# Reordering the chunk loop of RWKV-7 with a squared-ReLU FFN: state decay, state turn, squares and loads at other places in a slot

## The chip, the cores and the metric

The kernel runs on one core of a Trainium2 chip, in float32. The metric is the device time of one execution in microseconds (us). Five engines of the core work side by side, each through its own list of instructions in order: TensorE (PE, matrix products and transposes, with its weight loads as PEld), VectorE (DVE), ScalarE (ACT), GpSimd (POOL) and SyncE (SP, which here only issues DMA transfers). They wait for each other by semaphores.

## The reference

The first half is a recurrence over 768 time steps for 4 batches of 8 heads with 40 channels each; the second half is an FFN over the 3072 resulting rows of 320.

```python
for t in range(S):                       # per batch and head, state is D x D
    y[t]  = einsum('d,de->e', r[t], state)
    Sa    = einsum('de,e->d', state, a[t])
    state = state * w[t] - outer(Sa, b[t]) + outer(v[t], k[t])
x = y.transpose(0, 2, 1, 3).reshape(B * S, H * D)
h = maximum(x @ w_in, 0)                 # 320 -> 2048
out = (h * h) @ w_out                    # 2048 -> 320
```

## The kernel before

**Tiling.** Time is cut into chunks of 128 steps. There are 24 chunks, taken in the order "all four batches of chunk 0, then all four of chunk 1" and so on, so that neighbours in the order belong to different batches; `order[i]` holds batch and chunk. The main loop has one *slot* per chunk, numbered 0 to 23. In slot i three kinds of work are put side by side:

- the *chain* of chunk i (`chain`, L600): products of the state with the chunk's decayed a (first `xw`), a transpose, products with the inverse T and the block N, the new rows turned back, the growth of the state (`grown`, added by DVE in L662), the masked products RX, and the output y, which DVE scales into `tokens` (L683). From there it is regrouped by small SBUF-to-SBUF DMAs for the FFN.
- the *preparation of chunk i+1*: `turn_rv` transposes r and v; `make_rv` makes the products RV and masks them on DVE (L332); `turn_k` transposes k and scales it with the decay `dec` into `kvT` (L510); `decay_state` multiplies the state of chunk i+1's batch with the decay accumulated since (L533, L536); `turn_down` and `scale_kb` scale k and b (L551); `make_a` makes and masks the products A; `turn_state` transposes the state on PE (L561) and ACT copies it to `sd` (L563). The state decayed here belongs to another batch than the one that chain i grows.
- *early work on later chunks* (`early`, called through `prepare`): scans and reciprocals of the decays, products N, and their stores to DRAM (`kept_e`, `kept_d`, `kept_n`). It is present in slots 0 to 14 and gone from slot 15 on. POOL inverts the blocks of several chunks at a time (`solving`), loading `kept_d` and storing `kept_t`; its results come back as T.

Between these stand pieces of the FFN (`Ffn`): `thirds` and `whole` are the first product (w_third, w_in) with ReLU on ACT, `square` squares the hidden rows on DVE (L742), `make_quarter` is a quarter of the second product (w_out). In slot 4 alone the last weights are still being converted (`halves`, from `rounding`), using the same PSUM buffers (`ps_f`, two of them) as `thirds`; `extra` then places additional FFN pieces, in slot 4 only.

**What sets the order.** The order is written out by hand. Slots 0 to 3 weave generators in fixed proportions (`woven`, with `rest` for the next chunk). From slot 4 on `sorted_slot` (L909) lists the calls one by one; each `step` runs its calls and then lets stores that are due go out (`tick`). Every engine executes its instructions in the order of these calls. `ps_w`, a pool of four PSUM buffers, takes turns among all transposes and masked products; `ps_c`, with two, among the chain's.

**Loads.** SP issues in order. For chunk i+1 the keys k, the decays `dec` (634 KB from `kept_e`) and b are issued by `loads` at the head of slot i, r and v for chunk i+2 within it (`fetch_next`, L905). `dec` has two buffers, of which the one loaded was last read by DVE in L683; k, b and v have two each, r has one.

Of the kernel before, what the change touches and what calls it, by code (L numbers as in the profile page):

```python
# [11 lines left out]
Alu = mybir.AluOpType  # L12
# [5 lines left out]
def kernel(  # L18
# [73 lines left out]
    def new(name, shape, bufs):  # L92
        return work.tile(shape, FP32, tag=name, name=name, bufs=bufs)
# [413 lines left out]
    def turn_k(i, g):  # L507
        kT, kT_ = turned("kvT", 1), turn(g["x"]["k"])
        down = g["dec"][:, DOWN]
        nc.vector.tensor_tensor(kT, kT_, down[:, :, 1:C + 1], Alu.mult)  # L510
        g["kT"], g["ends"] = kT, new("ends", [128, NP], 2)
        nc.vector.tensor_copy(g["ends"], down[:, :, 0])

    def make_a(i, g):
        g["A"] = masked("A", 2, g["kT"], g["aT"])
# [1 line left out]
    def turn_rv(i, g):  # L517
        x_ = g["x"]
        while "v" not in x_:
            line.pop(0)[1]()  # L520
        g["rT"], g["vT"] = turned("rT", 2), turned("kvT", 1)
        p_, p2_ = turn(x_["r"]), turn(x_["v"])
        nc.scalar.copy(g["rT"], p_)
        nc.scalar.copy(g["vT"], p2_)
        g["v"] = x_["v"]

    def decay_state(i, g):
        bb, c = order[i]
        if c == 0:
            return  # L530
        st = states.tiles[bb]
        f_ = new("f", [128, NP], 1)
        nc.vector.tensor_tensor(f_, ended[bb], g["ends"], Alu.mult)  # L533
        for e in range(2):
            own_ = st[e * DP:(e + 1) * DP, :, e, :D]
            nc.vector.tensor_tensor(own_, own_, f_[e * DP:(e + 1) * DP].unsqueeze(2).to_broadcast([DP, NP, D]), Alu.mult)  # L536
# [32 lines left out]
    def rest(i, g):  # L569
        begin(i, g)  # L570
        yield
        yield
        turn_k(i, g)
        joining = inverses(i, g) if i else iter(())
        if soon(i):
            next(joining, None)
        yield
        make_a(i, g)
        yield
        turn_rv(i, g)  # L580
        yield
        decay_state(i, g)
        make_rv(i, g)
        if i and unit_of[i] < FINE:
            next(joining)
        yield
        turn_down(i, g)
        yield
        scale_kb(i, g)
        turn_state(i, g)  # L590
        yield
        yield from joining
        yield
# [6 lines left out]
    def chain(i, g):  # L600
        bb, c = order[i]
        st = states.tiles[bb]
        first, second_ = slice(0, HC), slice(HC, C)
        low, high = slice(0, DP), slice(DP, 128)

        xw = quads(psum(ps_c))
        for h, q, e, rows in heads:
            mm(xw[rows, q], g["v"][:, h, :], g["A"][e][:, q], h < 2)
        yield
        if c > 0:  # L610
            for q in range(NP):
                mm(xw[:, q], st[:, q].rearrange("p e d -> p (e d)"), g["aT"][:, q], False)
        xc = turned("xnT", 1)
        nc.scalar.copy(xc[low], xw[low])  # L614
        for n in range(2):
            nc.scalar.copy(xc[high, :, n * HC:(n + 1) * HC], xw[high, :, (1 - n) * HC:(2 - n) * HC])
        yield

        p_ = psum(ps_c)
        for q in range(NP):  # L620
            nc.tensor.matmul(p_[:, q * 128:(q + 1) * 128], xc[:, q], ident, start=q == 0, stop=True, is_transpose=True,  # L621
                             skip_group_check=True)
        x_ = p_.rearrange("t (h d) -> t h d", h=H)[:, :, :D]
        xr = new("xr", [128, H, D], 1)
        nc.scalar.copy(xr, x_)
        yield
        T, N = g["T"], g["N"]
        xn = minus_x.next()
        halves = (first, second_)

        def times_t(half):
            xs = psum(ps_c)[:, :NP * D].rearrange("p (q d) -> p q d", q=NP)
            for h, q, e, _ in heads:
                rows = halves[half ^ e]
                mm(xs[rows, q], T[rows, order_of(h)], xr[rows, h], h < 2)
            nc.scalar.copy(xn[halves[half], ::2, :D], xs[halves[half]])
            nc.scalar.copy(xn[halves[half], 1::2, :D], xs[halves[1 - half]])  # L637

        times_t(0)
        yield  # L640
        for h, q, e, _ in heads:
            mm(x_[halves[1 - e], h], N[:, order_of(h)], xn[first, h, :D], False)
        nc.scalar.copy(xr[second_, ::2], x_[second_, ::2])
        nc.scalar.copy(xr[first, 1::2], x_[first, 1::2])
        yield
        times_t(1)
        yield
        p_ = psum(ps_c)
        for q in range(NP):
            nc.tensor.transpose(p_[:, q * 128:(q + 1) * 128], pair(xn, q), ident)  # L650
        xT = turned("xnT", 1)
        nc.scalar.copy(xT, quads(p_))
        yield
        k_, b_, v_, rT = (g[x] for x in ("k", "b", "v", "rT"))
        if c < NCH - 1:
            grown = psum(ps_c)[:, :NP * 2 * D].rearrange("p (q d) -> p q d", q=NP)
            for l_, r_ in ((k_, v_), (b_, xn)):
                for q in range(NP):
                    mm(grown[:, q].rearrange("p (e d) -> p e d", e=2), pair(l_, q), r_[:, 2 * q:2 * q + 2, :D], l_ is k_ and q == 0)
            for e in range(2):  # L660
                rows = slice(e * DP, (e + 1) * DP)
                nc.vector.tensor_tensor(st[rows, :, e, :D], grown[rows, :, e * D:(e + 1) * D], st[rows, :, e, :D], Alu.add)  # L662
            ended[bb] = new(f"end{bb}", [128, NP], 1)
            nc.vector.tensor_copy(ended[bb], g["up"][:, :, C])
        yield
        rx = masked("RX", 2, xT, rT)
        yield

        y_ = quads(psum(ps_c))
        if c > 0:  # L670
            sd = g["sd"]
            for q in range(NP):
                mm(y_[:, q], sd[:, q].rearrange("p e d -> p (e d)"), rT[:, q], q == 0)
        yield
        for m_, rows in ((g["RV"], k_), (rx, b_)):
            for q in range(NP):
                for e in range(2):
                    mm(y_[e * DP:(e + 1) * DP, q], rows[:, 2 * q + e, :], m_[e][:, q], c == 0 and q == 0 and rows is k_)
        n = i % GB
        if n == 0:  # L680
            tokens[i // GB] = new("tokens", [128, NP, GB * C], 2)
        t_ = tokens[i // GB][:, :, n * C:(n + 1) * C]
        nc.vector.tensor_tensor(t_, y_, g["up"][:, :, :C], Alu.mult)  # L683
        if n == GB - 1:
            t_ = tokens[i // GB]
            for j, row, h, d, m_ in moves:
                at = (h % 2) * DP + d
                store(t_[row:row + m_, j], t_[at:at + m_, h // 2], 1)
            later(lambda: gathered.add(i // GB), 2)
        yield  # L690
# [214 lines left out]
    def fetch_next(i, *names):  # L905
        if i < len(order):
            loaded.setdefault(i, {}).update({nm: fetch(nm, {"k": k, "b": b, "r": r, "v": v}[nm], i) for nm in names})

    def sorted_slot(i, g, ch):  # L909
        j = i + 1  # L910
        more = j < len(order)
# [16 lines left out]
        def extra():  # L928
            if not begun:
                second.thirds()  # L930
                second.whole()

        halves = lambda: [next(rounded, None) for _ in range(2)] if not begun else None

        def loads():
            if more:
                fetch_next(j, "k")
                n["dec"] = kept_here[j % 2]
                nc.sync.dma_start(out=n["dec"][:USED], in_=kept_e[j])
                fetch_next(j, "b")  # L940

        loads()
        step(on(ch), halves)
        if more:
            begin(j, n)
# [3 lines left out]
            next(joining, None)  # L949
        fetch_next(j + 1, "r")  # L950
        step(second.make_quarter, halves)
        extra()
        step(on(ch))
        step(of(make_rv), second.thirds)
        step(on(ch), on(one), on(two), on(two))
        if fine:
            next(joining, None)
        step(second.whole, on(two))
        step(on(ch))
        step(on(one), of(turn_k))  # L960
        step(on(ch), of(decay_state), on(one), of(turn_down), of(scale_kb))
        step(on(ch), of(turn_state), second.square)
        if fine:
            next(joining, None)
        step(on(ch), of(make_a), second.thirds, on(one))
        fetch_next(j + 1, "v")
        step(second.whole, on(two), on(two))
        if not early_join:
            next(joining, None)
        step(on(ch), extra)  # L970
# [1 line left out]
        if more:  # L972
            later_chain = n["chain"] = chain(j, n)
            next(later_chain)
        run(ch)
        step(second.square, second.make_quarter)
        step(second.make_quarter, on(two))
        for gen in (one, two, joining):
# [2 lines left out]
    for i in range(len(order)):  # L981
# [4 lines left out]
        if i < B:  # L986
            woven(i, g, ch)
            n = ready[i + 1]
            n["chain"] = chain(i + 1, n)
            next(n["chain"])  # L990
            if i == B - 1:
                fetch_next(i + 2, "r", "v")
        else:
            sorted_slot(i, g, ch)
        while unit < len(units) and all(m_ in done for m_ in range(len(order)) if unit_of[m_] == unit):
# [46 lines left out]
```

## Time and profile before

| | |
|---|---|
| median of three runs | 1095.37 us (1087.47 to 1097.03) |
| profiled execution | 1094.95 us, span 1093.2 us |
| PE busy | 952.3 us, 87% of the span |
| PE weight loads (PEld) | 785.3 us, 72% |
| DVE busy | 491.6 us, 45% |
| ACT busy | 284.4 us, 26% |
| POOL busy | 669.4 us, 61% |
| DMA | 106.92 MB, mean 98 GB/s |
| TensorE clock granted, mean | 0.87 of full |

The profile is one execution. Busy time of PE is modelled at its ends, so a full PE can still hide some slack; the waits ahead of an instruction, and what released it, tell more than the sums. "PE ps_w L87" names matrix products into the buffers `ps_w`, issued by the helper in line 87; many products share that line and are told apart by their tiles. "DVE RX L332" after an arrow is what ended a wait. Slots 0 to 3 take the first 250 us or so, slots 4 to 14 run to about 725 us, slots 15 to 23 to about 1016 us, and the rest is FFN alone.

### The profile page before, as it was taken

The page shows a single profiled execution, that of the slowest core. Times are in us where ns is not written, and L with a number is a line of the kernel's source. Part 1 is how long each engine was busy: PE and PEld are TensorE (multiplying, and loading weights), DVE is VectorE, ACT ScalarE, POOL GpSimd, SP SyncE. Part 2 cuts the span into 40 slices and gives each one's busy share as a digit, 9 for nine tenths or more (in the row PEclk, how much of TensorE's full clock was granted, in tenths as well). Part 3 has the DMA queues.
Part 4 walks back from the last instruction along what each step waited for, and adds up shares of the span by engine and source line. Part 5 has one row for each costly group of instructions (what it writes and reads, how often), then busy time and mean ns, then how long its engine had stood idle before and what let it go on. Part 6 is the DMA issues. An engine that isn't in the chain of part 4 may idle for free.

```text
span 1093.2 us, 19699 instructions
## 1 busy us (share of the span) xinstructions
PE 952.3 (87%) x7728; PEld 785.3 (72%) x7728; DVE 491.6 (45%) x908; ACT 284.4 (26%) x643; POOL 669.4 (61%) x1128
## 2 busy tenths in 40 slices
PE   6275765685899899999899999999999999999998
PEld 5264654674788787778677877878888887777776
DVE  5456683784554435537246345344323433231111
ACT  3133241332231322222312222212222222322111
POOL 4788544886885399993699976999768810000000
PEclk8666575566998898999988998989999999999999
DMA  8878969678144862654873655541644314230000
GB/s 109 145 141 165 174 168 177 147 150 138 43 82 108 143 118 58 98 98 117 142 125 58 100 132 110 95 85 26 136 90 84 65 37 92 47 63 7 13 13 12
DMA packets 261376, 106.92 MB, mean 98 GB/s; under 512 B 244100, under 2 KB 250372, under 8 KB 259620
## 3 DMA queue, kind: packets, MB, share of 16 engines
q1 hardware_dynamic: 256756, 86.65, 44.4%
q0 software_dynamic: 3440, 18.88, 7.5%
q8 instruction: 61, 1.00, 0.4%
q10 hardware_dynamic: 1088, 0.13, 0.1%
q14 instruction: 31, 0.25, 0.1%
HBM read 72.47 MB, written 31.19 MB: 95 GB/s over the span
## 4 chain that ended last, share of the span: by engine, by line
PE 66%; DVE 12%; DMA 8%; issue 4%; ACT 4%; POOL 3%; SPq 2%; ACTq 0%; DVEq 0%; POOLq 0%
PE ps_f L87 36%; PE ps_c L87 13%; PE ps_w L87 11%; PE ps_w L316 4%; DMA in_w<-in_w_dram 2%; DMA dec<-kept_e 2%; DVE hid L742 1%; SPq L108 1%; DVE state L536 1%; PE ps_c L621 1%; POOL half_t L450 1%; POOL half_p L448 1%; DVE RX L332 1%; DMA blocks<-kept_t 1%; DVE kvT L510 1%
## 5 line engine op out<-in xcount | busy, mean ns | idle before, releaser
L448 POOL TENSOR_TENSOR half_p<-half_n,half_t 128x70 f32<-128x70 f32 (+52 forms) x502 | 296.7, 591 | 101.5 <-DMA half_n<-kept_d 51.8
L450 POOL TENSOR_TENSOR half_t<-half_t,half_p 128x70 f32<-128x70 f32 (+52 forms) x502 | 323.4, 644 | 39.3
L87 PE MATMUL ps_f<-w_out,hid 128*128 128x320 f32 x768 | 221.0, 438 | 0.0
L87 PEld LDWEIGHTS ps_f<-w_out,hid 128*128 128x128 f32 x768 | 142.0, 191 | 54.9 <-issue 4.4
L87 PE MATMUL ps_f<-tokens,w_in 128*128 128x256 f32 x672 | 172.7, 415 | 0.0
L87 PEld LDWEIGHTS ps_f<-tokens,w_in 128*128 128x128 f32 x672 | 136.2, 208 | 27.0 <-issue 5.6
L742 DVE TENSOR_TENSOR hid<-hid 128x512 f32<-128x512 f32 x96 | 83.4, 904 | 64.7 <-ACT hid L735 64.7
L332 DVE TENSOR_TENSOR RV<-ps_w,upper 128x512 f32<-128x512 f32 x48 | 30.9, 686 | 154.8 <-PE ps_w L87 154.8
L735 ACT ACTIVATE hid<-ps_f 128x512 f32<-128x512 f32 x84 | 50.2, 597 | 142.5 <-PE ps_f L87 142.5
L683 DVE TENSOR_TENSOR tokens<-ps_c,dec 128x512 f32<-128x512 f32 x24 | 16.6, 690 | 133.5 <-PE ps_c L87 133.5
L87 PE MATMUL ps_w<-decay,bT 40*128 40x128 f32 x352 | 42.1, 373 | 33.2 <-DVE decay L365 22.7
L87 PEld LDWEIGHTS ps_w<-decay,bT 40*128 40x128 f32 x352 | 36.0, 265 | 42.6 <-DVE RX L332 16.2
L87 PE MATMUL ps_f<-tokens,w_third 64*128 64x256 f32 x336 | 54.0, 427 | 6.3 <-DVE w_out L266 6.3
L510 DVE TENSOR_TENSOR kvT<-ps_w,dec 128x512 f32<-128x512 f32 x24 | 16.5, 686 | 86.0 <-ACT minus_x L637 54.1
L372 ACT COPY N<-ps_w 128x512 f32<-128x512 f32 x24 | 14.0, 585 | 147.5 <-PE ps_w L87 114.4
L614 ACT COPY xnT<-ps_c 64x512 f32<-64x512 f32 x24 | 13.9, 579 | 145.7 <-PE ps_c L87 145.6
L352 DVE TENSOR_TENSOR_SCAN decay<-ps_w,ones 128x64 f32<-128x64 f32 x88 | 23.8, 270 | 61.8 <-PE ps_w L316 56.7
L87 PEld LDWEIGHTS ps_f<-tokens,w_third 64*128 64x128 f32 x336 | 37.1, 214 | 9.2 <-DVE w_out L266 6.6
L87 PEld LDWEIGHTS ps_c<-xr,T 64*64 64x64 f32 x768 | 29.4, 146 | 19.6 <-issue 15.6
L87 PE MATMUL ps_w<-dec,kvT 40*128 40x128 f32 x384 | 38.6, 335 | 1.1 <-DVE in_b L551 0.9
L357 DVE RECIPROCAL decay<-decay 128x256 f32<-128x256 f32 x22 | 38.2, 1737 | 0.0
L358 DVE RECIPROCAL decay<-decay 128x256 f32<-128x256 f32 x22 | 37.3, 1696 | 0.0
(137 smaller groups left out, 1479.0 us busy)
## 6 DMA issues: line engine op xcount, KB each, us to landing
kept_e<-decay SPq DMA_DIRECT2D x22, 633.8 KB
dec<-kept_e SPq DMA_DIRECT2D x22, 633.8 KB
hid<-in_moe_w_out_dram SPq DMA_DIRECT2D x16, 320.0 KB
half_n<-kept_d POOLq DMA_DIRECT2D x6, 768.0 KB, 12.1
in_w<-in_w_dram SPq DMA_DIRECT2D x24, 160.0 KB
in_ab<-in_b_dram SPq DMA_DIRECT2D x24, 160.0 KB
in_ab<-in_a_dram SPq DMA_DIRECT2D x24, 160.0 KB
in_k<-in_k_dram SPq DMA_DIRECT2D x24, 160.0 KB
```

What stands on the lines that cost most here:

```text
L87: nc.tensor.matmul(o, l_, r_, start=start, stop=True, skip_group_check=True)
L316: nc.tensor.transpose(p_[:, q * 128:(q + 1) * 128], pair(x_, q), ident)
L332: nc.vector.tensor_tensor(t_, p_, over4(upper), Alu.mult)
L352: nc.vector.tensor_tensor_scan(up[:, q, MID + 1:C + 1], wT[:, q, MID:], ones, 1.0, Alu.mult, Alu.mult)
L357: nc.vector.reciprocal(down[:, :, MID + 1:C + 1], up[:, :, MID + 1:C + 1])
L358: nc.vector.reciprocal(up[:, :, :MID], down[:, :, :MID])
L448: nc.gpsimd.tensor_tensor(p_, part[:, at:at + m_].unsqueeze(1).to_broadcast([128, n, m_]), t3[:, :n, s:s + 1].to_broadcast([128, n, m_]), ...
L450: nc.gpsimd.tensor_tensor(t3[:, :n, s + 1:], t3[:, :n, s + 1:], p_, Alu.subtract)
L510: nc.vector.tensor_tensor(kT, kT_, down[:, :, 1:C + 1], Alu.mult)
L683: nc.vector.tensor_tensor(t_, y_, g["up"][:, :, :C], Alu.mult)
L735: nc.scalar.activation(h_, p_.rearrange("p f t -> p (f t)"), Act.Relu)
L742: nc.vector.tensor_tensor(h_, h_, h_, Alu.mult)
```

## The change

Six things are moved or replaced; no product or element of the result changes:

- `decay_state` reads the decay for the whole chunk straight from `dec`; the small copy `ends` (L512) is gone. In `sorted_slot` it is called before `make_rv` rather than after `turn_k`.
- The copy `end`, taken after the state has grown (L664), is made by ACT instead of DVE.
- `turn_state` and the first `second.square` of a slot come after `make_a` rather than before.
- `loads` becomes a function of its own. It is called at the end of slot i for chunk i+2, right after the chain, before the remaining stores of that slot are issued; before, the next slot's head called it. Its order is now `dec`, k, b rather than k, `dec`, b.
- At the end of slot 3 the order is `dec`, k, b, v; before it was r, v, k, `dec`, b. That r is now fetched within slot 3 by `rest`, right after the transposes that free its buffer.
- In slot 4 the first `extra` of FFN pieces is taken from its place after the second `make_quarter` and put after the chain's second product with T; the ordinary `thirds` of that slot is thereby the first FFN work.

As built, on SP the three loads stand ahead of the five stores of `kept_d` and `kept_n` in two places, between slots 5 and 6 and between slots 9 and 10; elsewhere only `dec` and k change places. On PE only the state's transposes move (behind the products of decay and bT, or of `w_third` where there are none), and slot 4's FFN.

```diff
         kT, kT_ = turned("kvT", 1), turn(g["x"]["k"])
         down = g["dec"][:, DOWN]
         nc.vector.tensor_tensor(kT, kT_, down[:, :, 1:C + 1], Alu.mult)
-        g["kT"], g["ends"] = kT, new("ends", [128, NP], 2)
-        nc.vector.tensor_copy(g["ends"], down[:, :, 0])
+        g["kT"] = kT
...
-        nc.vector.tensor_tensor(f_, ended[bb], g["ends"], Alu.mult)
+        nc.vector.tensor_tensor(f_, ended[bb], g["dec"][:, DOWN, :, 0], Alu.mult)
...
         turn_rv(i, g)
+        if i == B:
+            fetch_next(i + 1, "r")
         yield
...
-            nc.vector.tensor_copy(ended[bb], g["up"][:, :, C])
+            nc.scalar.copy(ended[bb], g["up"][:, :, C])
...
+    def loads(j):
+        if j < len(order):
+            n = ready.setdefault(j, {})
+            n["dec"] = kept_here[j % 2]
+            nc.sync.dma_start(out=n["dec"][:USED], in_=kept_e[j])
+            fetch_next(j, "k", "b")
+
...
-        def loads():
-            if more:
-                fetch_next(j, "k")
-                n["dec"] = kept_here[j % 2]
-                nc.sync.dma_start(out=n["dec"][:USED], in_=kept_e[j])
-                fetch_next(j, "b")
-
-        loads()
         step(on(ch), halves)
...
         step(second.make_quarter, halves)
-        extra()
-        step(on(ch))
+        step(on(ch), of(decay_state))
         step(of(make_rv), second.thirds)
         step(on(ch), on(one), on(two), on(two))
...
         step(second.whole, on(two))
+        step(on(ch), extra)
+        step(on(one), of(turn_k))
+        step(on(ch), on(one), of(turn_down), of(scale_kb))
         step(on(ch))
-        step(on(one), of(turn_k))
-        step(on(ch), of(decay_state), on(one), of(turn_down), of(scale_kb))
-        step(on(ch), of(turn_state), second.square)
...
         step(on(ch), of(make_a), second.thirds, on(one))
         fetch_next(j + 1, "v")
-        step(second.whole, on(two), on(two))
+        step(of(turn_state), second.square, second.whole, on(two), on(two))
...
         run(ch)
+        loads(j + 1)
         step(second.square, second.make_quarter)
...
             if i == B - 1:
-                fetch_next(i + 2, "r", "v")
+                loads(i + 2)
+                fetch_next(i + 2, "v")
```

## The prediction

> **What bounds the kernel now.** I read the page's slices first: where TensorE (PE) is full, and what clock it was granted.
>
> ```profile
> PE   6275765685899899999899999999999999999998
> PEclk8666575566998898999988998989999999999999
> ```
>
> From the twelfth slice on PE is at least 80%, mostly over 90% busy, so the later part is bound by PE. Its clock is not whole there, though: digits of 8 and 9 stand until slice 26 (to about 725 us), then only 9s. Busy time by stretch shows what that means. Columns: stretch, length, busy us of PE, weight loads, DVE, ACT and POOL, granted clock, DMA share, GB/s.
>
> ```profile
> 255.00:725.00 470.00, 433.11 (x3491) 360.12 (x3491) 227.94 (x401) 118.40 (x270) 364.10 (x472) 0.90 0.55 102
> 725.00:1008.00 283.00, 278.55 (x2411) 228.22 (x2409) 90.61 (x164) 73.87 (x168) 130.06 (x200) 1.00 0.35 68
> ...
> 332.80:343.00 10.20, 10.20 (x56) 8.96 (x54) 5.24 (x11) 1.91 (x5) 8.64 (x20) 0.50 0.35 88
> 421.50:431.70 10.20, 9.79 (x49) 7.79 (x47) 6.07 (x10) 1.68 (x4) 9.57 (x9) 0.50 0.32 84
> 592.20:602.40 10.20, 9.82 (x56) 8.21 (x54) 6.68 (x11) 1.69 (x5) 9.57 (x9) 0.50 0.29 75
> ```
>
> Between 255 and 725 us (slots 4 to 14, those that also prepare later chunks) PE stands idle 36.9 us and there are stretches at half clock; from 725 to 1008 it is idle 4.5 us and never halved. Next, what PE waited for in 255 to 725 (us in total, times, longest):
>
> ```profile
> PE ps_w L87 <- DVE RX L332: 9.9, 8, 3.5
> PE ps_c L561 <- DVE state L536: 9.4, 8, 1.7
> PE ps_w L545 <- DMA dec<-kept_e: 7.1, 2, 4.5
> PE ps_f L87 <- DVE w_out L266: 6.3, 1, 6.3
> PE ps_w L316 <- DMA in_w<-in_w_dram: 2.3, 1, 2.3
> ```
>
> The first two are one cause, DVE's order. The timeline of slot 8:
>
> ```profile
> 457.85 0.69 DVE L510 TENSOR_TENSOR kvT<-ps_w,dec 128x512 f32<-128x512 f32 x1 [2.66 <-ACT minus_x L637]
> 458.46 0.16 DVE L512 COPY ends<-dec 128x4 f32<-128x4 f32 x1
> 458.66 0.92 DVE L533 TENSOR_TENSOR f<-end,ends 128x4 f32<-128x4 f32 x1
> 459.62 1.49 DVE L536 TENSOR_TENSOR state<-state,f 64x160 f32<-64x160 f32 x2
> 461.13 0.69 DVE L364 TENSOR_TENSOR bT<-ps_w,decay 128x512 f32<-128x512 f32 x1
> 461.25 0.63 PE L561 MATMUL ps_c<-ident,state 128*128 128x128 f32 x4 [0.87 <-DVE state L536]
> ...
> 464.18 2.17 DVE L742 TENSOR_TENSOR hid<-hid 128x512 f32<-128x512 f32 x2
> 466.38 1.29 DVE L332 TENSOR_TENSOR RX<-ps_w,upper 128x512 f32<-128x512 f32 x2
> 467.13 1.75 PE L87 MATMUL ps_w<-decay,bT 40*128 40x128 f32 x16 [1.77 <-DVE RX L332]
> ```
>
> PE first waits for the state's decay before turning it, then for the RX masks, which stand behind two squares nobody needs yet. Slots 7, 11, 12 and 14 have the same pair, each followed by a half-clock stretch.
>
> **What the Trainium skill says.** "TensorE: Matmul & The Clock Gate", Part 1: PE's clock is halved after an idle window of about 3.4 us; its subsection "A second HAM failure mode" adds that frequent short idling also makes it oscillate. The trace agrees with the second: halvings of 3.4, 6.8 or 10.2 us follow gaps of only 1 to 2 us, while slot 9, with two gaps near 0.6 us (500 to 508 us, clock 1.00), has none. "SBUF — State Buffer", "two separate sides": a DVE operation with two SBUF inputs can be shut out by a GpSimd one; L536 indeed spreads from 316 to 1247 ns. "DMA: Bandwidth & Descriptors", "Queues, rings and completion order": a queue's descriptors are consumed in ring order, so a load behind a large one waits for it.
>
> **The change, part by part**, against the profiled execution: span 1093.2 us, 1094.95 us in all, 0.42 us under the median.
>
> 1. *State decay ahead of the RV masks; copy of the ends gone (L512); end copy on ACT.* Per slot 0.16 to 0.89 us of L512, 0.2 to 0.9 of L533 and two L536 of 0.57 leave the place behind kvT, about 2.1 us (2.57 in slot 8). They go where DVE idled 4.87 us for the RV products. The 20 end copies (0.33 each on DVE) cost ACT about as much; ACT is 26% busy and waits for nothing by them, so nothing. The copies of slots 0 to 3 (0.2 to 0.5 each) lie beside DMA waits: nothing either. In return f now waits for dec at the head of DVE's queue: RV masks, reciprocals and kvT stand behind it. Slot 8 has room: RV at 450.63, kvT at 457.85, the RX products may start about 460.4. After dec come f 0.17, state 1.14, RV 1.29, reciprocals 3.4, kvT and bT 1.4, together 7.4: dec may land 460.4 - 7.4 - 450.6 = 2.3 us after the RV products. It was issued at 444.20; a landing takes 6.62 us in slot 10's chain, so 450.8: inside.
> 2. *State's turn and squares behind the A masks.* PE no longer needs L536 there, the RX masks come 1.3 to 2.3 us (two squares) sooner. The squares are read only by the slot's end; sd is read after 16 matmuls of 3.72 us, which cover the turn and its 0.59 us copy.
>    Parts 1 and 2 together: of 9.9 + 9.4 us above, plus 2.0 us for L561 in the late slots, I keep back 0.4 for slot 5 (RX must still wait for bT), 1.6 for slot 13 and 1.0 for slot 10 (below): **-18.3**.
> 3. *Loads ahead of stores.* In slot 6 dec was issued at 359.13 behind eight token stores, five keeps and k, beside POOL's 1.5 MB load, and took 16.45 us. The keeps (1.83 + 0.61) and k (0.65) now come after: issue at about 355.6, landing at 6.62 about 362.2, before RV at 363.7: **-4.4**, PE's wait. In slot 10 issue 535.3, landing 541.9, 6.7 us after RV: PE's 2.5 us moves but stays. Slot 13: dec waits for the tokens multiply as before, so its issue (648.22) stays; beside POOL's load it may land anywhere from 654.8 to 668.7, where kvT did not wait; I keep its gap. POOL's take follows the keeps about 2 us later plus the 954 KB ahead of them; its solve ends at 498 and T is asked for at 519.5: covered.
> 4. *Slot 4.* r arrives a slot early: PE's 4.6 us for it goes. But v is now behind dec, k and b. v was used at 255.15; the three are 634 + 320 KB, at the 160 to 230 GB/s of that window 4 to 6 us. So v lands near 259.5, and scans and rounding behind it move too: **+4.5** (bounds +0, if the queue drains faster, and +7). FFN from step 5: the 6.3 us wait on w_out's rounding now has 16 xr,T (0.66) and 16 RV products (1.16) ahead: **-1.8**. The four squares ahead of RX (3.86 us) go, which the 3.5 us wait counted above.
> 5. *The clock.* Between 291.8 and 725.3 eleven halved stretches hold 81.7 us of busy PE. Eight w_out matmuls take 2.32 us at full clock and 4.01 halved, 16 A products 1.04 and 1.98: about 45% is loss, 36.8 us. The stretches at 527 (after in_w's wait, untouched), 551 and 677 (slots 10, 13) stay, 9.2 us. Of the other 27.6 I take three quarters, **-20.7**, since new waits near 1 us would bring some back; bounds 0 and -36.8.
>
> Sum: -18.3 - 4.4 + 4.5 - 1.8 - 20.7 = -40.7. 1094.95 - 40.7 = 1054.
>
> **Rivals.**
> *Gaps only (1075).* The halvings may come from the small products of these slots, not from the gaps. For: the same stretches always hold the bT products. Against: slot 9 has them too and no halving. Then -20.0: 1075, give or take 7.
> *Replaced waits (1092).* Every gap closed uncovers the next, as POOL's solves, in_w's loads (13.1 us in slot 9) or the bT multiply. For: POOL is 77% busy from 255 to 725. Against: T waits for POOL nowhere there, with 21 us or more to spare. Gain 0 to 6.
> *Slower: dec at DVE's head (1103).* If dec lands more than 2.3 us after the RV products in slots 6, 8, 10, 12, 13 and 14, f, state, RV and reciprocals (6.0 us) follow it where kvT alone did, 2.1 us of them saved: +3.9 each, +23.4, and their halvings stay. Slots 4, 7, 9 and 11 still give 8.4 in gaps and about 9.2 in clock; slot 4's loads add 2.7: +8.5. For: slots 6 and 10 were over the point, 8, 12 and 14 lie within 2 us of it. Against: dec goes out 0.65 to 3.5 us earlier.
>
> **Numbers.** Forecast 60% (1040 to 1067), gaps only 23% (1067 to 1082), replaced 9%, slower 8%. All gaps and the whole clock loss, with v free, would be about 1031. Range 1036 to 1082. About 1% either way is what a measurement of this kernel tells from no change (its three runs span 0.9%): faster 0.84, same 0.08, slower 0.08.
>
> **What the profile after would show.** No wait of L561 on L536; RX masks not preceded by squares; clock 1.00 through slots 7, 8, 11, 12 and 14; PE idle in 255 to 725 reduced from 36.9 to under 20 us; in slot 4 PE waiting for in_v, not in_r. Wrong would be: DVE waiting on dec at L532 in many slots, or halved clock with no gap before it.

## The result: 1040 us, and where the profile shows the gain

The changed kernel takes 1040.15 us (median of four runs, 1038.23 to 1040.43), the kernel before beside it 1091.42 us (four runs, 1078.75 to 1097.03): ratio 0.9554, 95% interval 0.9516 to 0.9592. The forecast was 1054 us with a range of 1036 to 1082, so sign and range held; but two of its terms were wrong by 15 to 20 us and partly cancelled: that the range held is luck in part. The profiled execution of the changed kernel took 1038.23 us (span 1036.5), 56.7 us less than the profiled one before. Medians below are over all runs of a kernel; ratios leave disturbed runs out, so the two can differ a little.

The page's slices of the changed kernel, PE and its granted clock:

```profile
PE   6465664684799999999599999999999999999998
...
PEclk9666565656799999999699999999999999999999
```

Where digits of 8 stood up to slice 27 (the prediction says 26), there are only 9s of the clock from slice 12 on, with one hole: slice 20 (busy 5, clock 6). To see it by slot I cut both traces where DVE writes the slot's `tokens`. First three slots of the kernel before (slots 7, 8 and 10), then the same slots and the stretch of slots 15 to 23 after. Columns as in the prediction: stretch, length, busy us of PE, PEld, DVE, ACT and POOL, granted clock, DMA share, GB/s.

```profile
394.30:436.60 42.30, 40.19 (x316) 33.29 (x314) 20.61 (x33) 10.10 (x23) 39.48 (x37) 0.88 0.45 78
436.60:477.10 40.50, 37.57 (x318) 31.12 (x316) 20.83 (x34) 10.10 (x23) 37.83 (x35) 0.96 0.51 90
...
515.70:565.70 50.00, 43.85 (x332) 35.26 (x330) 18.59 (x33) 11.69 (x27) 37.00 (x50) 0.86 0.75 136
```

```profile
377.30:411.60 34.30, 34.30 (x316) 29.22 (x314) 18.46 (x31) 10.10 (x24) 31.55 (x36) 1.00 0.64 106
411.60:446.00 34.40, 34.40 (x317) 29.32 (x314) 19.84 (x31) 10.11 (x24) 32.28 (x28) 1.00 0.60 111
...
482.60:538.20 55.60, 41.52 (x332) 34.46 (x330) 18.15 (x31) 11.70 (x28) 41.52 (x65) 0.82 0.67 138
...
678.10:961.70 283.60, 280.57 (x2441) 230.63 (x2435) 92.44 (x153) 74.71 (x173) 157.33 (x223) 1.00 0.36 67
```

Slots 7 and 8 are now PE-bound without a remainder: 34.3 us long, 34.3 us busy, clock 1.00. Slot 10 became *longer*. All slots together, in us:

| slots | before | after | difference | PE busy | PE idle | prediction |
|---|---|---|---|---|---|---|
| 0 to 3 | 239.6 | 240.2 | +0.6 | | | 0 |
| 4 | 65.2 | 64.0 | -1.2 | -3.8 | +2.6 | -0.8 |
| 5 to 9 and 11 to 14 | 375.5 | 318.3 | **-57.2** | -38.7 | -18.5 | **-37.9** |
| 10 | 50.0 | 55.6 | **+5.6** | -2.3 | +7.9 | **0** |
| 15 to 23 | 288.1 | 283.6 | -4.5 | -2.8 | -1.7 | -2.0 |
| FFN alone after them | 74.8 | 74.8 | 0 | | | 0 |

(The last column sorts the terms of the prediction by slot: 4.5 - 1.8 - 3.5 in slot 4; 18.3 less the 3.5 of slot 4 and the 2.0 of the late slots, plus 4.4 and 20.7, in the nine; 1.1 of the 20.7 belong to the halved stretch at 291.8, in slot 4.)

What PE waits for after, 255 to 680 us, the same slots that the 255 to 725 us of the prediction held; in us in total, times, longest:

```profile
PE ps_w L316 <- DMA in_v<-in_v_dram: 12.8, 1, 12.8
PE ps_c L87 <- DMA tokens<-tokens: 12.8, 1, 12.8
PE ps_f L87 <- DVE w_out L266: 3.9, 1, 3.9
PE ps_w L87 <- DVE kvT L510: 2.0, 2, 1.1
PE ps_w L87 <- DVE in_b L550: 1.3, 4, 0.3
```

The waits for RX, for the state's decay and for `dec` (9.9, 9.4 and 7.1 us before) are gone. Three single waits are left: v in slot 4, w_out in slot 4, and one in slot 10 that did not exist. The timeline of slot 8, where the pair of gaps was read before:

```profile
432.88 0.69 DVE L510 TENSOR_TENSOR kvT<-ps_w,dec 128x512 f32<-128x512 f32 x1 [1.06 <-PE ps_w L316]
...
433.48 0.68 DVE L364 TENSOR_TENSOR bT<-ps_w,decay 128x512 f32<-128x512 f32 x1
...
435.32 1.16 PE L87 MATMUL ps_w<-rT,xnT 40*128 40x128 f32 x16
...
436.51 1.29 DVE L332 TENSOR_TENSOR RX<-ps_w,upper 128x512 f32<-128x512 f32 x2 [0.39 <-PE ps_w L87]
...
437.72 1.28 DVE L332 TENSOR_TENSOR A<-ps_w,upper 128x512 f32<-128x512 f32 x2
...
438.07 1.06 PE L87 MATMUL ps_w<-decay,bT 40*128 40x128 f32 x16
...
438.91 2.45 DVE L743 TENSOR_TENSOR hid<-hid 128x512 f32<-128x512 f32 x2
439.06 0.66 PE L560 MATMUL ps_c<-ident,state 128*128 128x128 f32 x4
```

bT follows kvT at once, no copy, f or state between; DVE idles 0.39 us until the RX products are done and masks them at once; the squares stand behind the A masks; the state's turn (L560) waits for nobody. And the new wait of slot 10:

```profile
493.86 2.32 PE L87 MATMUL ps_f<-w_out,hid 128*128 128x320 f32 x8
...
494.61 0.60 POOL L453 DMA_DIRECT2D kept_t<-half_t  x1 [0.30 <-POOL half_t L450]
495.22 1.03 POOL L420 DMA_DIRECT2D half_n<-kept_d  x2
...
499.93 1.32 SPq L464 DMA_DIRECT2D T<-kept_t  x2
...
509.01 1.08 PE L87 MATMUL ps_c<-xr,T 64*64 64x40 f32 x16 [12.82 <-DMA tokens<-tokens]
```

POOL's solve of chunks 10 to 13 ends at 494.6; its result is stored, T is loaded at 499.93 behind the 1.5 MB that POOL fetches for its next solve, and PE starts at 509.0. The profile puts the wait down to a `tokens` DMA, the last semaphore to come; what the products read is T, and the experiment on the solve below shows that it is T. The clock is halved for 20.5 us from 499.2 on.

### The profile page after: what moved, and what is told of

It is laid out like the page before. It is cut to its first block, busy times and chain, and to the rows that moved or that the text cites. A ratio compares the mean times of both kernels' runs of the same rounds, so it can differ in the third digit from the quotient of the medians.

```text
span 1036.5 us, 19696 instructions
## 1 busy us (share of the span) xinstructions
PE 907.5 (88%) x7728; PEld 756.3 (73%) x7728; DVE 484.4 (47%) x864; ACT 285.2 (28%) x663; POOL 672.7 (65%) x1128
## 4 chain that ended last, share of the span: by engine, by line
PE 57%; POOL 14%; DMA 11%; DVE 5%; ACT 4%; issue 4%; SPq 4%; ACTq 0%; POOLq 0%; DVEq 0%
PE ps_f L87 30%; PE ps_c L87 12%; PE ps_w L87 9%; POOL half_t L450 7%; POOL half_p L448 6%; PE ps_w L316 3%; SPq L108 2%; DMA in_v<-in_v_dram 2%; DMA blocks<-kept_t 2%; DMA dec<-kept_e 1%; DMA half_n<-kept_d 1%; DMA kept_t<-half_t 1%; PE ps_c L651 1%; PE ps_c L560 1%; DMA in_k<-in_k_dram 1%
## 5 line engine op out<-in xcount | busy, mean ns | idle before, releaser
L87 PE MATMUL ps_f<-tokens,w_in 128*128 128x256 f32 x672 | 158.7, 390 | 0.0
L87 PEld LDWEIGHTS ps_f<-tokens,w_in 128*128 128x128 f32 x672 | 127.5, 195 | 18.4 <-issue 1.0
L743 DVE TENSOR_TENSOR hid<-hid 128x512 f32<-128x512 f32 x96 | 88.8, 961 | 49.7 <-ACT hid L736 49.7
L532 DVE TENSOR_TENSOR f<-end,dec 128x4 f32<-128x4 f32 x20 | 7.1, 355 | 112.1 <-DMA dec<-kept_e 112.1
L87 PE MATMUL ps_w<-decay,bT 40*128 40x128 f32 x352 | 31.9, 327 | 23.2 <-DVE decay L365 21.3
L332 DVE TENSOR_TENSOR RV<-ps_w,upper 128x512 f32<-128x512 f32 x48 | 30.9, 686 | 42.4 <-PE ps_w L87 41.9
L87 PE MATMUL ps_f<-tokens,w_third 64*128 64x256 f32 x336 | 47.0, 391 | 3.9 <-DVE w_out L266 3.9
L87 PE MATMUL ps_c<-xr,T 64*64 64x40 f32 x768 | 35.7, 242 | 15.2 <-DMA tokens<-tokens 12.8
L87 PEld LDWEIGHTS ps_w<-decay,bT 40*128 40x128 f32 x352 | 29.2, 231 | 26.7 <-issue 14.7
L332 DVE TENSOR_TENSOR RX<-ps_w,upper 128x512 f32<-128x512 f32 x48 | 30.9, 686 | 26.9 <-PE ps_w L87 26.8
L357 DVE RECIPROCAL decay<-decay 128x256 f32<-128x256 f32 x22 | 38.2, 1737 | 0.0
```

The costliest lines, as they stand in the source:

```text
L87: nc.tensor.matmul(o, l_, r_, start=start, stop=True, skip_group_check=True)
L332: nc.vector.tensor_tensor(t_, p_, over4(upper), Alu.mult)
L357: nc.vector.reciprocal(down[:, :, MID + 1:C + 1], up[:, :, MID + 1:C + 1])
L743: nc.vector.tensor_tensor(h_, h_, h_, Alu.mult)
```

## The experiments

All edits are to the changed kernel (1040.15 us). Each edited kernel was run four times, beside the kernel before; differences are between medians, "gap" is PE idle time, "the front" is how far PE has come in the slots. The changed kernel was not run again beside them, and the medians of the kernel before were 1088.1 to 1091.6 us in these sessions, so differences under some 4 us say nothing. For the two smallest gains below, v first and the early work, the ranges of the runs lie apart from the changed kernel's, but the 95% intervals of the ratios overlap with its own: they are less sure than the rest.

### The two moves on DVE, each undone

```diff
-        step(on(ch), of(decay_state))
+        step(on(ch))
...
-        step(on(ch), on(one), of(turn_down), of(scale_kb))
+        step(on(ch), of(decay_state), on(one), of(turn_down), of(scale_kb))
```

> The changed kernel with the state's decay put back behind turn_k (it still reads dec itself; everything else as changed). Theory (the decay's place closes PE's waits and with them the halved clock): DVE's chain kvT, f, state, bT is about 1.7 us longer again in slots 5 to 14, the RX products wait for bT, some of the halvings come back: 10 to 22 us slower than the changed kernel, near 1050 to 1062. Rival (the squares' place alone makes the gain): within 3 us of 1040.

Measured: 1054.74 us (1050.46 to 1055.57), ratio 0.9655 [0.9592, 0.9718]: **+14.6**, as the theory had it. The timeline of slot 7 of this kernel shows how a short block on DVE costs more than itself:

```profile
404.91 0.91 DVE L532 TENSOR_TENSOR f<-end,dec 128x4 f32<-128x4 f32 x1
...
405.85 1.41 DVE L535 TENSOR_TENSOR state<-state,f 64x160 f32<-64x160 f32 x2
...
407.27 0.69 DVE L364 TENSOR_TENSOR bT<-ps_w,decay 128x512 f32<-128x512 f32 x1
...
408.02 1.04 PE L87 MATMUL ps_w<-rT,xnT 40*128 40x128 f32 x13 [0.78 <-DVE bT L364]
```

f and state (2.3 us, spread wide here) push bT back, the RX products need the PSUM buffer that bT is read from, and PE stops for 0.78 us; 1.4 us later, at 409.4, the clock is halved for 10.2 us. Six slots have such a gap of 0.48 to 1.36 us ahead of or in the RX products, 5.5 us in all, and each is followed by 3.4 or 10.2 us at half clock; so are two of only 0.17 and 0.32 us in slot 12 (3.4 us). Slot 10, with 1.9 us ahead of the keys' transposes and 0.4 us at RX, has none.

```diff
-        step(on(ch))
+        step(on(ch), of(turn_state), second.square)
         if fine:
...
-        step(of(turn_state), second.square, second.whole, on(two), on(two))
+        step(second.whole, on(two), on(two))
```

> The changed kernel with turn_state and the first square put back ahead of make_a. Theory: the RX masks stand behind 1.3 to 3.9 us of squares again, PE waits for them in slots 4, 8, 12 and 13 at least, with a halving each: 8 to 18 us slower than the changed kernel, near 1048 to 1058; L560 on PE waits for nothing, since the state was decayed earlier. Rival (the decay's place alone makes the gain): within 3 us of 1040.

Measured: 1053.79 us (1049.52 to 1061.54), ratio 0.9662 [0.9589, 0.9736]: **+13.6**, again the theory. PE waits for the RX masks in nine slots:

```profile
PE ps_w L87 <- DVE RX L332: 10.2, 9, 1.8
...
PE ps_c L87 <- DMA T<-kept_t: 4.4, 1, 4.4
```

In both kernels the wait of slot 10 for T has shrunk or gone: a slower front comes to T later. So each undone move costs more than its 14 us in the slots where it acts, and slot 10 gives part of it back.

Both undone at once (the two diffs together):

> Both put back: only the loads, slot 4's FFN, the end copy on ACT and the missing ends copy remain of the change. Theory: most of the gain is lost, 1080 to 1092, since POOL's late T costs nothing once PE is slow again and the loads give about 4 us in slot 6 and lose about 5 in slot 4. Rival (loads make the gain): near 1050.

Measured: 1070.56 us (1068.77 to 1074.14), ratio 0.9815 [0.9739, 0.9891]: **+30.4**, about the sum of the two (28.2). The theory's 1080 to 1092 missed. The remaining parts (order of loads, slot 4, the copies) are worth some 20 us alone (12 to 28 by the interval), where 1080 to 1092 leaves them at most 11:

```profile
PE ps_w L87 <- DVE RX L332: 15.7, 11, 2.8
PE ps_w L316 <- DMA in_v<-in_v_dram: 9.7, 1, 9.7
PE ps_c L560 <- DVE state L535: 5.0, 8, 1.1
```

The DVE gaps are back, 20.7 us where L332 and L536 made 19.3 before; but slot 6 has a gap of 0.4 us and no halving left (4.5 us of wait for `dec` and 13.7 us at half clock before), and the seven halved stretches from 290 us on hold 37.4 us against 85 us in eleven before. By the two traces slot 6 is 8.9 us shorter than in the kernel before, slot 13 5.0 and slot 10 3.7, while slot 4 is 6.4 longer. Gaps of the same sum were followed by shorter halvings here; the count by windows below bears on that.

### The new wait of slot 10

```diff
-        for s in range(size - 1):
+        for s in range(size - 1 if u != 6 else size // 2):
             if s in between:
```

> The changed kernel with POOL's solve of the unit of chunks 10 to 13 cut to half of its steps, so that part of the inverse for these four chunks is left out. Theory (PE's 12.8 us wait in slot 10 is for T, which comes late because POOL finishes at 494.6): the wait goes, and with it the halved stretch of 20 us that follows it (about 10 us busy, 45% lost): 14 to 18 us faster than the changed kernel, near 1023 to 1026. Rival (the wait is for the token stores and their DMA, which the trace names as its releaser): within 3 us of 1040.

Measured: 1023.71 us (1021.65 to 1028.07), ratio 0.9384 [0.9321, 0.9448]: **-16.4**, the theory's 14 to 18. So slot 10 hangs on POOL's solve. A smaller wait came into view in its place, on DVE and then on PE:

```profile
505.11 0.62 DVE L532 TENSOR_TENSOR f<-end,dec 128x4 f32<-128x4 f32 x1 [13.01 <-DMA dec<-kept_e]
...
506.95 1.29 DVE L332 TENSOR_TENSOR RV<-ps_w,upper 128x512 f32<-128x512 f32 x2
507.70 1.11 PE L316 MATMUL ps_w<-ident,in_k 128*128 128x128 f32 x4 [4.04 <-DVE RV L332]
```

f, at DVE's head, waits for `dec`; the RV masks stand behind it and hold the PSUM buffer of the next transposes. That is the mechanism of the prediction's slower rival, in one slot.

Can T be had sooner without cutting work? POOL's solve starts when the last `kept_d` of its four chunks is stored, and it waits for that in the changed kernel (POOL, slot 6):

```profile
POOL half_n L420 <- DMA kept_d<-N: 13.8, 1, 13.8
```

Two ways to start it sooner. First, the stores ahead of the loads:

```diff
         run(ch)
-        loads(j + 1)
...
         for gen in (one, two, joining):
             run(gen)
+        loads(j + 1)
```

> The changed kernel with the three loads issued at the very end of a slot, behind kept_d and kept_n (dec still ahead of k): the part 'ahead of the slot's stores' undone. Theory (the loads delay kept_d, so POOL's solve of chunks 10 to 13 starts later and T is late by as much): POOL starts 5 to 7 us earlier, PE's wait in slot 10 shrinks by as much, dec is 3 us later in slots 6 and 10, which costs 0 to 3: 2 to 7 us faster, near 1036. Rival (loads ahead of stores are what slot 6 gains by): slot 6 gets its wait for dec and a halving back, 5 to 9 us slower, near 1047.

Measured: 1039.63 us (1037.56 to 1043.88), ratio 0.9563 [0.9509, 0.9617]: no change. POOL fetched at 355.8 instead of 359.8, but this solve ended no sooner (495.4 against 494.6; why it took longer is open). PE's gap before T fell from 12.8 to 5.9 us only because PE came to it later: b, one of the loads now behind, held DVE and PE in slot 6 (a 1.6 us gap, 10.2 us halved). Slot 10 also got two gaps of 1.8 and 1.2 us behind T and a second halving. So neither expectation holds. The trace is of the slowest of the four runs (1043.88): in it slot 6 is 7.5 us longer than in the changed kernel's and slot 10 as long (55.6). The other three were 3 to 6 us faster, and no trace shows where.

Second, the early work on chunk 12 in slot 4, where PE waits anyway, not in slot 5:

```diff
-    ahead = {0: (4, 5), 1: (6, 7), 2: (8, 9), 3: (10,), 4: (11,), 5: (12, 13)}
+    ahead = {0: (4, 5), 1: (6, 7), 2: (8, 9), 3: (10,), 4: (11, 12), 5: (13,)}
```

> The changed kernel with the early work on chunk 12 in slot 4 (beside 11) rather than in slot 5 (beside 13), so that the last kept_d of chunks 10 to 13 is written in the middle of slot 5. Theory (slot 10 waits for POOL): POOL starts this solve about 14 us earlier, right after its last one, and PE does not wait for T in slot 10; slot 4 has room while it waits for v and the rounding: 12 to 19 us faster, near 1025. Rival (slot 4 grows by what slot 5 loses and POOL is bound elsewhere): within 4 us of 1040.

Measured: 1032.88 us (1031.22 to 1033.74), ratio 0.9491 [0.9434, 0.9549]: **-7.3**, short of the theory's 12 to 19. The solve ended at 477.3 and the wait for T went; part was lost again to the other mechanism, f ahead of the RV masks in slots 6 and 10, with halvings of 10.2 and 13.7 us:

```profile
PE ps_w L316 <- DMA in_v<-in_v_dram: 12.6, 1, 12.6
PE ps_w L316 <- DVE RV L332: 4.5, 2, 3.5
```

### The order of v in slot 4

```diff
-                loads(i + 2)
                 fetch_next(i + 2, "v")
+                loads(i + 2)
```

> The changed kernel with v fetched ahead of dec, k and b at the end of slot 3. Theory (v is late because it lies behind 954 KB in its queue): PE's 12.8 us wait for in_v in slot 4 shrinks to about 7, everything after moves with it: 4 to 6 us faster, near 1035. Rival (v's landing is bound by its own issue or by other traffic; or the time comes back in slot 10, where T decides): within 2 us of 1040.

Measured: 1035.06 us (1032.46 to 1036.51), ratio 0.9513 [0.9463, 0.9563]: **-5.1**. The prediction had 4.5 us for v behind the three loads. PE's wait for v is 6.7 us here, 12.8 in the changed kernel's trace (9.4 to 13.3 in the experiments that keep its order):

```profile
PE ps_c L87 <- DMA T<-kept_t: 14.4, 1, 14.4
PE ps_w L316 <- DMA in_v<-in_v_dram: 6.7, 1, 6.7
```

Slot 10 took most of the gain back, as the second half of the rival had it: slot 9 ended 8.2 us sooner than in the changed kernel's trace (474.4 against 482.6), slot 10 only 1.9 us sooner. T came sooner too, for the solve ended at 488.1 and not 494.6, but PE still waited longer for it, and a second halved stretch of 10.2 us followed. Another 2.4 us between the two traces lie in slot 14, where the gap of the changed kernel is missing here; so v's own share of the 5.1 us is uncertain.

### Does a short gap halve the clock by itself?

Slots 16 to 21 have no early work and no gap over 0.3 us. There I made gaps of 1.9 us by letting ACT copy a buffer onto itself, first ahead of the chain's last transpose:

```diff
+        for _ in range(3 if 16 <= i < 22 else 0):
+            nc.scalar.copy(g["rT"], g["rT"])
         times_t(1)
```

> The changed kernel with three copies of rT onto itself (0.58 us each on ACT) ahead of the second product with T in slots 16 to 21, which run at full clock with PE never waiting: they delay the copies that PE's turn of minus_x waits for, so each of the six slots gets one gap of about 1.7 us on PE and nothing else. Theory (a gap of 1 to 2 us brings a halved stretch of 3.4 to 10 us, of which 45% is lost): 6 x (1.7 + 1.5 to 4.6), 19 to 38 us slower than the changed kernel, near 1060 to 1078. Rival (halving comes from the small products of the slots with early work, not from gaps): 6 x 1.7, about 10 us slower, near 1050, clock 1.00 from 700 to 920 us.

Measured: 1053.33 us (1049.65 to 1058.47), ratio 0.9687 [0.9628, 0.9746]: +13.2, against 11.5 us of gaps: under the theory's 19, a little over the rival's 10. The trace has the six gaps, all of 1.91 us, and one halving. The two lines are the stretch that begins with the fourth gap, and the halved one after the fifth:

```profile
833.20:845.00 11.80, 9.92 (x88) 9.05 (x89) 6.56 (x11) 3.79 (x9) 10.54 (x17) 1.00 0.09 15
...
871.00:877.80 6.80, 6.80 (x47) 5.79 (x46) 4.17 (x7) 0.59 (x1) 0.00 (x0) 0.50 0.01 2
```

So "a gap of 1 to 2 us halves the clock", on which my clock term stood, falls as a general sentence. Then the same gap in the place where the kernels with halvings have it, right ahead of the RX products:

```diff
         xT = turned("xnT", 1)
+        for _ in range((6 if i < 20 else 4) if 16 <= i < 22 else 0):
+            nc.scalar.copy(g["rT"], g["rT"])
         nc.scalar.copy(xT, quads(p_))
```

> Leaves nothing of the kernel out: in slots 16 to 21 ACT copies rT onto itself (six times in slots 16 to 19, four times in 20 and 21, 0.59 us each) ahead of its copy of xT, so that PE finds a gap of about 1.9 us right before the RX products in each of six slots without early work. Theory 'place': it is a gap ahead of the RX products (followed by kvT, third and state products of 40 and 64 rows) that halves the clock, in whichever slot; each of six gaps then brings a halved stretch of about 10 us with some 4.6 us lost, 1065 to 1080 us against 1040 after. Rival 'neighbourhood': the halvings need the early work of slots 4 to 14 (bT products, scans' transposes) around the gap; here the gaps alone count, six times 1.9 less what little slack there is, with one or two halvings: 1050 to 1056 us.

Measured: 1059.37 us (1056.31 to 1067.0), ratio 0.9695 [0.9628, 0.9762]: between the two expectations, so neither holds whole. Four gaps of 1.54 us and two of 1.99 us; after three of them the clock was halved, for 3.4, 6.8 and 3.4 us. One gap without and one with a halving:

```profile
806.70:820.00 13.30, 11.76 (x122) 10.35 (x122) 7.00 (x11) 3.34 (x7) 12.03 (x17) 1.00 0.12 19
...
875.80:882.60 6.80, 6.80 (x42) 5.69 (x40) 3.78 (x6) 0.59 (x1) 0.00 (x0) 0.50 0.01 2
```

The sum agrees: 10.1 us of gaps, 13.6 us at half clock after them, and 6.8 more in slot 14 (after its gap of 1.06 us, where the changed kernel has 1.15 us and no halving), at the 45% of the prediction 9.2 us, make 19.3 of the 20.0 us between the two profiled executions. So place may count (three of six against one of six, too few to be sure), and what the slot holds besides seems to: with the decay late, the gaps at RX of 0.48 to 1.36 us in six slots with early work were all followed by halvings. And slot 14 shows that much the same gap goes either way.

The kept traces hold an answer to much of this. In all 14 of them (both kernels and the twelve edits) the clock changes only on a fixed grid of 3.41 us: every stretch at one clock between its first and its last change is a whole multiple of it. So the work of PE can be counted window by window. Let a matmul weigh the columns that it streams, times the share of the 128 rows and of the 128 columns of the array that it fills: 128 columns with 40 rows weigh 40, with 128 rows 128. The fullest windows come to about 4100 at full clock and 2050 at half clock. Windows below about 1510 were followed by a window at half clock, windows above it by one at full clock, in 4133 of 4173 cases (in 406 of them the clock changed). Sorted by PE's busy time alone, at the best threshold, 352 cases come out wrong instead of 40; by the columns alone, 335.

This sorts the cases above. The windows that the six gaps of 1.91 us fell into held 1904, 1824, 1664, 1584, 1104 and 1440, and the fifth was followed by half clock (the sixth is one of the 40). With the gap at RX the three slots that were halved have a window of 1120, 1216 and 1280, the other three none below 2000. Slot 14 has 1576 in the changed kernel and 1488 here. So a gap counts by how it falls on the grid, and by what stands beside it: between thin products, of 40 or 64 rows, a window falls below 1510 sooner than between wide ones. It also gives a reason for long halvings: a window at half clock must reach 1510 of some 2050 to end one. The weights and the threshold are fitted to these traces after the runs; no run was predicted with them.

### Towards a better version

Must f stand ahead of the RV masks, or is ahead of kvT enough?

```diff
-        step(on(ch), of(decay_state))
+        step(on(ch))
...
-        step(on(one), of(turn_k))
+        step(on(one), of(decay_state), of(turn_k))
```

> Decay of the state between RX's neighbours and RV: it is called right ahead of turn_k, so on DVE f and state stand behind the RV masks and reciprocals but still ahead of kvT, where DVE idled 2.7 us before the change. Theory: only the place behind kvT hurt (14.6 us when undone); here f's wait for dec holds back only kvT, which waits for dec itself, and 1.3 us of f and state fit DVE's idle time there. So the same as the changed kernel or a few us better, 1035 to 1042 us, and no wait of RV masks for f in slots 6 and 10. Rival: DVE is full between RV and kvT in the slots with early work, and f and state push kvT, scale_kb and RX back by about 1.3 us each in some slots, with halvings: 1047 to 1056 us.

Measured: 1039.36 us (1036.55 to 1042.1), ratio 0.9506 [0.9438, 0.9574]: the same as the changed kernel. Not by the theory alone, though: gaps of 1.3 and 1.4 us ahead of RX came in slots 5 and 9, each with 10.2 us halved, as the rival said; they were paid for by the gap before T, which fell to 6.2 us. With the wait for T smaller, the place ahead of kvT is the better one, as the last run shows.

The early work in slot 4 and v first, together:

> Two edits that helped alone, together: v fetched ahead of dec, k and b at the end of slot 3 (-5.1 us alone), and early work on chunk 12 in slot 4 rather than slot 5 (-7.3 us alone). They act on different waits (in_v in slot 4; POOL's T in slot 10). Theory: they add, 1027 to 1029 us. Rival: in_v's wait hides part of the added work of slot 4, so that v sooner brings nothing there: 1032 to 1034 us.

Measured: 1031.05 us (1028.6 to 1034.38), ratio 0.9428 [0.9369, 0.9487]: not told apart from the early work alone, and the theory's full sum is not there. In this execution the solve ended at 483.1, not 477.3, slot 10 waited 9.4 us for T again, and v left 6.8 us.

With the decay right ahead of kvT as well (all three diffs):

> The two edits of the run before, and the decay of the state right ahead of turn_k rather than ahead of the RV masks. With chunk 12 prepared in slot 4, PE waited in slots 6 and 10 for RV masks that stood behind f's wait for dec: 2.1 and 3.5 us of gaps and 24 us at half clock (about 11 lost). Theory: these go when f no longer stands ahead of the RV masks, 1012 to 1020 us. Rival: dec is late in those slots anyway, kvT and the keys' scaling wait for it, and the gap only moves to the RX or A products and halves there: 1025 to 1030 us.

Measured: **1022.72 us** (1019.2 to 1025.27), ratio 0.9348 [0.9291, 0.9404], the fastest here that does all the work: 17 us faster than the changed kernel, 8 us than the one without the third edit. It is 3 us over the theory's range, below the rival's. Waits, 240 to 725 us:

```profile
PE ps_f L87 <- DVE w_out L266: 3.9, 1, 3.9
PE ps_w L316 <- DMA in_v<-in_v_dram: 3.9, 1, 3.9
PE ps_c L87 <- DMA T<-kept_t: 3.1, 1, 3.1
PE ps_w L87 <- DVE kvT L510: 1.9, 1, 1.9
```

RV is gone from the list; f waits for `dec` 3.0 us in slot 10, but with the RV masks done. The kvT line is slot 9, the price of the later f that the run before had shown.

## Why the prediction came out as it did

**Parts 1 and 2, DVE's order: right.** The gaps they were to close are closed; undone, each costs 14 us and both 30 (with the halvings that come back). For the nine slots with early work outside slots 4 and 10, the predicted gap terms come to 17.2 us (12.8 and the 4.4 of `dec`), and PE's idle time fell by 18.5. The end copies on ACT were not tried alone; at 26 to 28% busy ACT shows no wait from them. The sign I named for this part going wrong was a poor one: DVE waits for `dec` at L532 seven times, 52.3 us in 255 to 700, but next to none of it holds PE. It bites in slot 10, when T's wait no longer covers it, and in slot 6 when POOL's fetch is early; the slower rival is a real mechanism, confined to those two.

**Part 5, the clock: right in kind, the size wrong, and the reason too simple.** Of 36.8 us I took 20.7. Every halved stretch after slot 4 went except the new one of slot 10, also those at 527, 551 and 677 us that I had left in. In the nine slots the halved stretches had held 64.8 us of busy PE, by 45% 29 us of loss; busy time fell by 38.7. So the halved stretches gave 8 us more than the 20.7 I counted, and another 9.5 us of busy time went that 45% of them does not explain: slots 8 and 12 lost 3.1 us of busy time each with only 3.4 us halved. In slot 8 it can be placed: 1.9 us lie on the w_in products, most of them in the halved stretch, and 1.0 us on the products of kvT and bT beside the RX wait, where matmuls start up to 0.4 us apart and the view counts most of that as busy; so part of this "clock" gain is probably DVE's order again. And the general reason, that a gap of 1 to 2 us brings a halving, did not survive the made gaps: 1 of 6 and 3 of 6. The rival "gaps only", with halvings from the small products alone, is refuted by slots 7 and 8, which have all those products at clock 1.00. What fits the runs is that gap and thin products act together, through the work that is left in a window of 3.41 us; the windows need not be idle.

**Part 3, the step that failed: "its solve ends at 498 and T is asked for at 519.5: covered".** Both numbers are the kernel before's:

```profile
498.28 0.60 POOL L453 DMA_DIRECT2D kept_t<-half_t  x1 [0.30 <-POOL half_t L450]
...
519.55 6.53 SPq L464 DMA_DIRECT2D T<-kept_t  x2
```

The second is SP's issue of T's load; PE came to its first product with T at 533.4. The end of the solve was near (494.6 after). But I set it against the *old* time at which T is asked for, while my own terms for slots 4 to 9 bring that some 24 us forward (an estimate: 0.8 in slot 4, about 11.5 of gaps and 12 of clock), to before the end of the solve. In fact slot 9 ended 33 us sooner, and PE reached its product with T at 496.2. And the end of the solve is not T: the store takes 5.3 us to land and the load 9.1 us, 14.4 us together. The solve did not move along with the front: after slot 5 SP took 6.25 us to issue the four `kept_d` behind the loads, 1.83 before, and POOL fetched them at 359.8 as it had at 359.5, though slot 5 ended 6.8 us sooner. The cost is the run with the short solve: 16.4 us. The third rival was dismissed on the same number ("with 21 us or more to spare"); it holds in one slot, and there takes a quarter of what the change would have gained (16.4 of 51.3 + 16.4). It fits that undoing either part costs just 14 us.

The same part also took its gain too small. POOL's fetch now comes after `dec`, not beside it: `dec`, issued at 349.9, had its last packet at 355.2, where it had taken 16.5 us. With both DVE moves undone, slot 6 alone kept 8.9 us where 4.4 were forecast, and loads, slot 4 and copies together about 20. Which of them gives the rest was not taken apart.

**Part 4, slot 4: right in its terms, the sum in part by luck.** Predicted -0.8 in all, measured -1.2. PE used v at 260.5 where 259.5 was forecast, and w_out's wait fell by 2.4 where 1.8 was taken. But PE's idle time rose by 2.6 us, and busy time fell by 3.8: of the 23.9 us at half clock in this slot in both kernels PE is busy for 16.0 before and 10.6 after, since more of them lie over the wait for v. Hardly any term stood for that (1.1 us of part 5).

**Balance.** Nine slots 19 us better than forecast, slot 10 5.6 worse, the late slots 2.5 better: 16 us better in the profiled execution, 14 in the median. Without the loss in slot 10 it would have been about 1024, below the range. PE idle in slots 4 to 14 after 255 us came to 26.2 us and not "under 20"; without the wait for T it is 13.4.

## What to carry to other kernels

An engine off the critical path that works at its own pace, as POOL here, has slack only against a front that stands still: subtract the gains you expect ahead of that point, and add what lies between the engine's end and the consumer (store, load, and what is queued with them). A short block on an in-order engine is cheap or dear by what stands directly behind it; 1.3 us of decay per slot cost nothing in the sum ahead of kvT, and 14 us in all behind it. And when a change closes gaps, look for the next one where a producer's end time did not move; here it was single and large.

## What was not expected of the hardware

Half clock for much longer than the gap ahead of it: in slots with early work 0.48 us of idle PE was followed by 3.4 us, 0.78 us by 10.2 us, while five of six gaps of 1.91 us among the wide products of the late slots were followed by none, as were three of six gaps of 1.5 to 2.0 us ahead of the 40-row RX products. Counted by windows of 3.41 us on a fixed grid, and weighed by rows as above, 4133 of 4173 windows fit one threshold, about 1510, some 37% of the fullest.

A load behind a large fetch from another engine's queue: T's load was issued at 499.93 and its packets ran from 505.8 on, when the 1.5 MB that POOL had fetched (499.1 to 506.5) was nearly through. Whether the one held up the other, no run here tests.
